# Ten weight blocks decoded later and one at a time, and the low halves of split weights pinned to VectorE, in an attention, mixture-of-experts and feed-forward kernel

## The chip, the cores and the metric

One core of one Trainium2 chip. The metric is the time of one execution in microseconds (us), taken on the device; lower is better. Three timed runs of the kernel before gave 780.74, 778.58 and 780.11 us, median 780.11 us.

The engines that matter here: TensorE (PE, with its weight loads as PEld), VectorE (DVE), ScalarE (ACT), GpSimd (POOL), and the DMA queue that SyncE (SP) issues.

## The reference, cut to what matters

Three stages in a row: clustered attention, a top-1 mixture of experts (MoE), and a dense two-layer block with the activation `h * tanh(softplus(h))`. The change touches only the last one.

```python
def _moe2_setup():
    n_tokens, d_model, d_ff = (1536, 512, 2048)
    return {..., 'w_in': np.random.randn(d_model, d_ff).astype(np.float32) * (1.0 / np.sqrt(d_model)),
                 'w_out': np.random.randn(d_ff, d_model).astype(np.float32) * (1.0 / np.sqrt(d_ff))}

def _moe2_ref(x, w_in, w_out):
    h = x @ w_in
    sp = np.where(h > 20.0, h, np.log1p(np.exp(np.minimum(h, 20.0))))
    g = h * np.tanh(sp)
    return (g @ w_out).astype(np.float32)
```

The product with a numpy scalar makes `w_in` and `w_out` 64-bit floats, so the kernel has to turn them into 32-bit floats itself: that is the decode of which this document speaks.

## The kernel before, in words

**The last part.** The hidden width of 2048 is cut into 16 chunks of 128 columns (`F2 = 16`), and the 1536 tokens into two halves of 768. That makes 32 steps, n = 0 to 31; step n works on chunk `fc = n % 16` of half `n // 16`. Chunk fc has two weight blocks of 128x512, `WD[fc][0]` (from `w_in`) and `WD[fc][1]` (from `w_out`). Each step has, on the different engines:

- `f_split`: each of its two blocks is split into a high and a low part. ScalarE casts the block to `wh` (L1291), then the low part is `wl = WD - wh` (a subtraction recorded at the helper's line L1238). `wh` and `wl` come from the pools `mwh0` and `mwh1`, four pairs each.
- `f_in`, twice (i = 0, 1, for 384 tokens each): 12 matmuls into a PSUM tile `fps` (L1691); then the activation as a chain between VectorE and ScalarE: L1706 (VectorE, reads `fps`), L1709 (ScalarE, exp), L1712 (VectorE), L1717 (ScalarE, ln), L1720 (VectorE, reads `fps` for the last time), L1723 (ScalarE, exp), L1727 (VectorE, multiplies), L1730 (ScalarE, casts to the high half of `g`), L1238 (VectorE, `g` low half). There are two `fps` tiles, so TensorE can begin `f_in` i of step n+1 only when L1720 of `f_in` i of step n is done.
- `f_out`: 18 matmuls of 128x512 from `g`, `wh` and `wl` into six accumulators `ops` (L1766).

TensorE runs them in the order `f_in`(n+1, 0), `f_in`(n+1, 1), `f_out`(n).

**The decode.** A block (`d_block`) is loaded by a DMA that SP issues (L1516, tile `draw`, three buffers), scaled on GpSimd (L1521), its magnitude taken on ScalarE (L1527), then three instructions on VectorE (L1534 clamp, L1540 shifts, L1547 sign merged in), and one addition on GpSimd (L1554) that writes `WD`. There are 32 blocks. The first 22 (`NB = 22`) are decoded while the attention and MoE parts still run; blocks 22 to 31, that is chunks 11 to 15, are decoded inside the last part, since `WD` has memory of its own for only 11 chunks, and chunks 11 to 15 use buffers that become free when the MoE part is done.

**What sets the order.** A planner (`Plan`) lays out all instructions with due times (`at2`) and estimated durations, and writes every engine's queue in that order; each queue is then run strictly in order. An instruction may have alternatives (`alts`): the planner then picks the engine that it thinks finishes first. `sub` is the helper that makes the subtractions; without `psum=True` it offers VectorE and GpSimd. `split` passes `psum=key[0] != "f"`, so for the last part's weights either engine may be chosen.

Of the kernel before, what the change touches and what calls it, by code (L numbers as in the profile page):

```python
# [28 lines left out]
NB = 22  # L29
# [7 lines left out]
def f32(ap):  # L37
    return ap.bitcast(F32)
# [117 lines left out]
def t_dve(n):  # L156
    return 68 + 1.042 * n


def t_pool(n):  # L160
    return 40 + 2.33 * n
# [7 lines left out]
def cluster_attention__then__moe__then__act_mish_kernel(  # L169
# [103 lines left out]
    for i, cc in enumerate(CAPS):  # L273
# [5 lines left out]
        out=kcaps, in0=caps, scalar1=float(E), scalar2=float(E), op0=ALU.mult, op1=ALU.add  # L279
# [21 lines left out]
    for j in range(2):  # L301
        for part, src in ((0, chi), (1, clo)):
            c0 = part * 32 + j * 16
            nc.vector.tensor_copy(
                out=cbig[64 * j:64 * j + 64, :, c0:c0 + 16],
# [6 lines left out]
    for i in range(2):  # L312
        nc.sync.dma_start(
            out=xw[64 * i:64 * i + 64, :, D:], in_=w_gate.rearrange("(h d) e -> d h e", d=D)
# [503 lines left out]
    key = rp.tile([128, E], F32, name="key")  # L818
# [411 lines left out]
                    )  # L1230
                    rest(at_r, at_c, e, px, pw, ps1, ps2)

    def sub(out, in0, in1, deps, n, psum=False, pool=False, **kw):

        def f(eng="dve"):
            e = nc.vector if eng == "dve" else nc.gpsimd
            a, b_, c = out(), in0(), in1()
            e.tensor_tensor(out=a, in0=b_, in1=c, op=ALU.subtract)  # L1238
        alts = [("dve", t_dve(n))] * (not pool) + [("pool", t_pool(n))] * (not psum)
        return O(None, 0, f, deps, alts=alts, **kw)  # L1240

    moe = scope()
# [39 lines left out]
            ms["ld", s, fc, a] = o  # L1282
            after = [ms[0]["ld", t] for t in range(3)] + [o] if (s, fc) == (0, 0) else [o]

    def split(a, key, src, dep, prev, rel=(), pool=False):

        y = ms["wh", key, a] = [None, None]

        def act():
            y[0], y[1] = (mwh[a].tile([128, 512], F32R, tag=x, name=x) for x in ("wh", "wl"))  # L1290
            nc.scalar.copy(out=y[0], in_=src())  # L1291

        o = ms["sa", key, a] = O("act", 520, act, [dep, prev], acq=[(f"mwh{a}", key)])
        ms["sp", key, a] = sub(
            lambda: y[1], src, lambda: f32(y[0]), [o], 512, psum=key[0] != "f", rel=rel, pool=pool,
        )

    def e_split(s, fc):
        for a in range(2):
            if ms[s]["full"]:  # L1300
                ms["sp", (s, fc), a] = ms["ld", s, fc, a]
                continue
            split(a, (s, fc), lambda a=a: ms["w", s, fc, a], ms["ld", s, fc, a],
                  ms["sa", (s, fc), 0] if a else None, [(f"mwr{a}", (s, fc))])

    def e_xt(s, t):
# [29 lines left out]
        if z["full"]:  # L1336
# [3 lines left out]
        o = O("act", t_act(DC * n), lambda: nc.scalar.copy(  # L1340
            out=z["xh"][:, :, t0:t0 + n], in_=y["ps"]), [o])
        z["xt", t] = sub(
            lambda: z["xl"][:, :, t0:t0 + n], lambda: y["ps"],
            lambda: f32(z["xh"][:, :, t0:t0 + n]), [o], DC * n, psum=True, rel=[R],
# [228 lines left out]
    def at2(n, off=0.0):  # L1573
        plan.key = base_k + n * TS + off
# [5 lines left out]
    for n, (s, fc) in enumerate(steps):  # L1580
# [16 lines left out]
        if fc == NF - 1:  # L1597
            if s == 0:
                at2(5)
                o = O("dve", 1000, starts, [begun], after=[ms[0]["y", 2]])  # L1600
# [13 lines left out]
    for blk in range(NB):  # L1614
        if blk < ND0:
            n = (2 * blk + 1) * NF0 // (2 * ND0)
        else:
            n = NF0 - 1 + (blk - ND0) * (NS - 3 - NF0) // (NB - ND0)
# [10 lines left out]
    for b in range(B):  # L1629
# [36 lines left out]
        out=ids, in_=ids_d[:, 0:1].rearrange("(t p) o -> p (t o)", p=128)), ci + [ms[E - 1]["mm1", 0]])  # L1666
# [7 lines left out]
    def f_split(n):  # L1674
        half, fc = divmod(n, F2)
        for a in range(2):
            split(a, ("f", n), lambda a=a: WD[fc][a], dd[2 * fc + a], fs["hold"])
            fs["hold"] = ms["sa", ("f", n), a]

    def f_in(n, i):  # L1680
# [48 lines left out]
        def e8():  # L1729
# [14 lines left out]
        o = O(None, 0, e7, [o, o1], alts=[("dve", t_dve(384)), ("pool", t_pool(384))])  # L1744
        o = O("act", 413, e8, [o])
        fs["e", n, i] = sub(
            lambda: y["gl"], lambda: y["t"], lambda: f32(y["gh"]), [o], 384, rel=[W]
        )
# [69 lines left out]
    for n in range(NM):  # L1818
        at2(n - 2, 1.0)
        f_split(n)  # L1820
        if n < NM - 2:
            for i in range(2):
                at2(n - 1, 2.0 * i)
                f_in(n, i)

            for blk in range(NB, 2 * F2):
                if int((blk - NB) * 0.65 + 2) == n:
                    at2(n - 1, 2.5)
                    d_block(blk, [fs["in"]])
            f_out(n)  # L1830
# [41 lines left out]
```

## Time and profile before

| | |
|---|---|
| median of three runs | 780.11 us (778.58 to 780.74) |
| the profiled execution | 783.48 us |
| its span, first to last instruction | 781.5 us |
| mean granted TensorE clock over the span | 0.975 |
| TensorE busy | 746.9 us (96% of the span) |
| VectorE busy | 565.2 us (72%) |
| ScalarE busy | 476.8 us (61%) |
| GpSimd busy | 232.3 us (30%) |
| last part | about 491 to 774 us of the span |
| decode of blocks 22 to 31 on VectorE | 516 to 572 us of the span |

The shares of the whole span mix stages with different limits. The stage that the change touches has to be read by itself, step by step: a step of the last part begins, in this text, where VectorE starts L1706 of `f_in`(n, 0), and it ends where the next one starts.

Times of instructions include a tail of about 0.08 us that the next instruction on the same engine overlaps; what an instruction takes of a queue is the distance from its start to the start of the next, which is called its slot here.

### The profile page before, as it was taken

What the parts mean: (1) busy time and instruction counts of PE and PEld (TensorE: products, weight loads), DVE (VectorE), ACT (ScalarE), POOL (GpSimd) and SP (SyncE); (2) the same over time, 40 slices, a digit from 0 to 9 for tenths busy, and PEclk for the clock granted to TensorE, in tenths of its full rate; (3) what the DMA queues carried; (4) which work ended last, traced back from release to release, by engine and by line L of the source; (5) the groups of instructions that cost most, each with busy time, mean ns of one, the idle gap of its engine ahead of it and who ended that gap; (6) DMA issues with size and microseconds to landing.
All of it is one profiled execution on the core that took longest, in us unless ns stands there. A gap on an engine that the chain in (4) does not pass through costs nothing.

```text
span 781.5 us, 14002 instructions
## 1 busy us (share of the span) xinstructions
PE 746.9 (96%) x4809; PEld 707.7 (91%) x4810; DVE 565.2 (72%) x1114; ACT 476.8 (61%) x1053; POOL 232.3 (30%) x457
## 2 busy tenths in 40 slices
PE   7999999999999959999999999999899999999995
PEld 6999999999999958999999999988679999999894
DVE  6697887888888855787533333599987778777763
ACT  3587878878788864556433232565556666665644
POOL 2225345358543340144223333125420011000003
PEclk9699999999999988999999999999999999999998
DMA  8949486474541028778688999212100001000002
GB/s 177 216 97 227 113 227 145 136 164 147 117 101 34 1 95 259 229 195 238 206 258 269 300 308 287 78 55 81 55 1 0 1 20 63 0 1 1 1 1 81
DMA packets 96082, 97.34 MB, mean 125 GB/s; under 512 B 33053, under 2 KB 76061, under 8 KB 94981
## 3 DMA queue, kind: packets, MB, share of 16 engines
q1 hardware_dynamic: 92133, 88.91, 41.9%
q0 software_dynamic: 2304, 7.08, 2.4%
q8 instruction: 40, 0.66, 0.4%
q10 hardware_dynamic: 1568, 0.39, 0.3%
q14 instruction: 37, 0.30, 0.1%
HBM read 63.59 MB, written 12.32 MB: 97 GB/s over the span
## 4 chain that ended last, share of the span: by engine, by line
PE 27%; issue 26%; DVE 5%; POOL 1%; DMA 1%; ACT 1%; SPq 0%; POOLq 0%
PE hps L1366 6%; PE yps L1427 6%; PE hps L1350 5%; PE yps L1350 5%; PE fps L1691 2%; PE ops L1766 1%; POOL out_dram L1797 1%; DVE dm L1547 1%; DVE ft L1712 1%; PE tps L1326 1%; DVE ft L1727 1%; DMA wr<-in_moe_w_dram 1%; DVE ft L1706 1%; DMA win<-xs_dram 1%; DVE g L1238 0%
## 5 line engine op out<-in xcount | busy, mean ns | idle before, releaser
L1766 PE MATMUL ops<-wh,g 128*128 128x512 f32 x384 | 125.0, 392 | 0.7 <-ACT g L1730 0.7
L651 DVE TENSOR_REDUCE mn<-sps 128x1 f32<-128x768 f32 x96 | 91.4, 954 | 24.7 <-PE sps L644 23.5
L689 ACT CAST ph<-pt 128x512 fp32r<-128x512 f32 x144 | 81.8, 590 | 29.5 <-PE pt L680 28.7
L692 DVE TENSOR_TENSOR pl<-pt,ph 128x512 fp32r<-128x512 f32 x144 | 95.0, 684 | 5.2 <-ACT ph L689 3.7
L1691 PE MATMUL fps<-YH,wh 128*128 128x384 f32 x256 | 88.8, 347 | 7.9 <-DVE ft L1720 7.9
L655 ACT ACTIVATE p<-sps,mn 128x768 f32<-128x768 f32 x96 | 87.4, 911 | 3.4 <-DVE mn L651 2.9
L1691 PE MATMUL fps<-YL,wh 128*128 128x384 f32 x256 | 87.2, 340 | 0.0
L1691 PE MATMUL fps<-YH,wl 128*128 128x384 f32 x256 | 87.1, 340 | 0.0
L1766 PEld LDWEIGHTS ops<-wh,g 128*128 128x128 f32 x384 | 72.4, 189 | 16.1 <-ACT g L1730 1.1
L680 PE MATMUL pt<-ident,p 128*128 128x128 f32 x576 | 79.1, 275 | 0.4 <-ACT o L787 0.4
L1766 PE MATMUL ops<-wl,g 128*128 128x512 f32 x192 | 75.3, 392 | 0.0
L640 PE MATMUL sps<-asm 128*128 128x384 f32 x192 | 73.9, 385 | 0.0
L680 PEld LDWEIGHTS pt<-ident,p 128*128 128x128 f32 x576 | 68.4, 143 | 2.9 <-ACT o L787 0.5
L1797 POOL DMA_INDIRECT out_dram<-fo,ids x12 | 12.0, 1004 | 188.5 <-ACT fo L1791 120.7
L644 PE MATMUL sps<-asm 80*128 80x384 f32 x192 | 66.8, 348 | 0.0
L1717 ACT ACTIVATE ft<-ft,two 128x384 f32<-128x384 f32 x64 | 39.5, 617 | 41.5 <-DVE ft L1712 41.5
L1366 PE MATMUL hps<-xf,wr 128*128 128x232 f32 (+4 forms) x320 | 59.5, 329 | 1.4 <-DMA wr<-in_moe_w_dram 1.4
L1709 ACT ACTIVATE ft<-ft 128x384 f32<-128x384 f32 x64 | 33.6, 524 | 44.0 <-DVE ft L1706 43.7
L1691 PEld LDWEIGHTS fps<-YH,wh 128*128 128x128 f32 x256 | 48.8, 191 | 12.3 <-DVE ft L1720 11.4
L1554 POOL TENSOR_TENSOR WD<-dm,draw 128x512 int32<-128x512 int32 x32 | 42.5, 1330 | 55.1 <-DVE dm L1547 49.2
L1427 PE MATMUL yps<-hf,wr 128*128 128x232 f32 (+4 forms) x320 | 58.8, 327 | 0.0
L1238 DVE TENSOR_TENSOR wl<-WD,wh 128x512 fp32r<-128x512 f32 x56 | 38.5, 688 | 25.6 <-ACT wh L1291 25.5
(190 smaller groups left out, 1767.2 us busy)
## 6 DMA issues: line engine op xcount, KB each, us to landing
wr<-in_moe_w_dram SPq DMA_DIRECT2D x128, 256.0 KB
asm<-raw SPq DMA_DIRECT2D x16, 576.0 KB
draw<-in_moe_w_in_dram SPq DMA_DIRECT2D x16, 512.0 KB
draw<-in_moe_w_out_dram SPq DMA_DIRECT2D x16, 512.0 KB
asm<-raw SPq DMA_DIRECT2D x16, 384.0 KB
xs_dram<-zrow SPq DMA_DIRECT2D x16, 256.0 KB
vl<-in_v_dram SPq DMA_DIRECT2D x8, 384.0 KB
asm<-raw SPq DMA_DIRECT2D x16, 192.0 KB
```

Of the source, the lines that this page charges most:

```text
L640: nc.tensor.matmul(ps[:, half, :384], a[:, 1, c * 128:(c + 1) * 128], a[:, 0, sl], start=True, stop=False,)
L644: nc.tensor.matmul(ps[:, half, :384], a[:80, 2, c * 128:(c + 1) * 128], a[:80, 3, sl], start=False, stop=True,)
L651: nc.vector.tensor_reduce(out=y["mn"], in_=y["ps"][:, :, :384], axis=AX.XY, op=ALU.min)
L655: nc.scalar.activation(out=p.rearrange("p (a b) -> p a b", a=2), in_=y["ps"][:, :, :384], func=AF.Exp, bias=y["mn"], scale=-1.0, accum_out ...
L680: nc.tensor.transpose(ps[:, kk * 256 + u * 128:kk * 256 + u * 128 + 128], z["p", u][:, kc * 128:(kc + 1) * 128], ident,)
L689: nc.scalar.copy(out=v("ph"), in_=y["ps"])
L692: nc.vector.tensor_tensor(out=v("pl"), in0=y["ps"], in1=f32(v("ph")), op=ALU.subtract)
L1350: nc.tensor.matmul(ps, l, x[:, i], start=first and n == 0, stop=last and n == 2)
L1366: nc.tensor.matmul(ps, w[:, k * 128:(k + 1) * 128], z["x"][:, k, :cap], start=k == 0, stop=k == DC - 1,)
L1427: nc.tensor.matmul(z["y"][d], w[:, d * 128:(d + 1) * 128], h, start=fc == 0 and d % yd == 0, stop=fc == NF - 1 and (d + 1) % yd == 0,)
L1691: nc.tensor.matmul(ps[:, :384], l, r[:, k, c0:c0 + 384], start=(k == 0 and m == 0), stop=(k == DC - 1 and m == 2),)
L1766: nc.tensor.matmul(fs["o", t], l[:, sl], r, start=(fc == 0 and m == 0), stop=(fc == F2 - 1 and m == 2),)
```

## The change

Two edits. The ten blocks inside the last part were placed at step `int((blk - 22) * 0.65 + 2)`, that is at steps 2, 2, 3, 3, 4, 5, 5, 6, 7, 7; now at `int((blk - 22) * 1.2 + 2)`, steps 2, 3, 4, 5, 6, 8, 9, 10, 11, 12. And `split` always passes `psum=True`, so that `wl` is always made by VectorE. (The argument `pool` that goes away was never set.)

```diff
-    def sub(out, in0, in1, deps, n, psum=False, pool=False, **kw):
+    def sub(out, in0, in1, deps, n, psum=False, **kw):
...
-        alts = [("dve", t_dve(n))] * (not pool) + [("pool", t_pool(n))] * (not psum)
+        alts = [("dve", t_dve(n))] + [("pool", t_pool(n))] * (not psum)
...
         ms["sp", key, a] = sub(
-            lambda: y[1], src, lambda: f32(y[0]), [o], 512, psum=key[0] != "f", rel=rel, pool=pool,
+            lambda: y[1], src, lambda: f32(y[0]), [o], 512, psum=True, rel=rel,
         )
...
             for blk in range(NB, 2 * F2):
-                if int((blk - NB) * 0.65 + 2) == n:
+                if int((blk - NB) * 1.2 + 2) == n:
                     at2(n - 1, 2.5)
                     d_block(blk, [fs["in"]])
```

VectorE's queue in step 4, where before two blocks are decoded and now one; `dm` is the block in decode, `ft` the activation's tile, `fps` the PSUM tile. Before:

```order
L1540 TENSOR_SCALAR dm<-dm 128x512
L1706 TENSOR_SCALAR ft<-fps 128x384
L1547 SCALAR_TENSOR_TENSOR dm<-draw,dm 128x512
L1534 TENSOR_SCALAR dm<-dm 128x512
L1712 SCALAR_TENSOR_TENSOR ft<-ft 128x384
L1540 TENSOR_SCALAR dm<-dm 128x512
L1706 TENSOR_SCALAR ft<-fps 128x384
L1547 SCALAR_TENSOR_TENSOR dm<-draw,dm 128x512
L1720 TENSOR_TENSOR ft<-fps,ft 128x384
L1712 SCALAR_TENSOR_TENSOR ft<-ft 128x384
```

The last two instructions of one block and all three of the next stand among the activation's here. The same place now:

```order
L1540 TENSOR_SCALAR dm<-dm 128x512
L1706 TENSOR_SCALAR ft<-fps 128x384
L1547 SCALAR_TENSOR_TENSOR dm<-draw,dm 128x512
L1238 TENSOR_TENSOR wl<-WD_0_4674,wh 128x512
L1712 SCALAR_TENSOR_TENSOR ft<-ft 128x384
L1706 TENSOR_SCALAR ft<-fps 128x384
L1720 TENSOR_TENSOR ft<-fps,ft 128x384
L1712 SCALAR_TENSOR_TENSOR ft<-ft 128x384
```

The second block's three instructions are gone from between the first L1706 and the first L1720, and the `wl` of chunk 7, which GpSimd made, stands there instead.

GpSimd's queue in the last part, from the first `wl` on; `draw` is a loaded block, `WD_7545` and the like are decoded blocks. Before:

```order
L1238 TENSOR_TENSOR wl<-WD_0_4668,wh 128x512
L1521 TENSOR_SCALAR draw<-draw 128x512 x2
L1238 TENSOR_TENSOR wl<-WD_0_4672,wh 128x512
L1554 TENSOR_TENSOR WD_7545<-dm,draw 128x512
L1554 TENSOR_TENSOR WD_7567<-dm,draw 128x512
L1521 TENSOR_SCALAR draw<-draw 128x512 x2
L1238 TENSOR_TENSOR wl<-WD_0_4674,wh 128x512
L1554 TENSOR_TENSOR WD_7638<-dm,draw 128x512
L1554 TENSOR_TENSOR WD_7661<-dm,draw 128x512
```

Each `wl` stands between a pair of L1521 and the L1554 that write the decoded blocks. The same place now:

```order
L1521 TENSOR_SCALAR draw<-draw 128x512
L1554 TENSOR_TENSOR WD_7543<-dm,draw 128x512
L1521 TENSOR_SCALAR draw<-draw 128x512
L1554 TENSOR_TENSOR WD_7622<-dm,draw 128x512
L1521 TENSOR_SCALAR draw<-draw 128x512
L1554 TENSOR_TENSOR WD_7705<-dm,draw 128x512
```

The eight `wl` have left the queue (they stand in VectorE's now), and L1521 and L1554 alternate instead of coming in pairs. SP's queue of DMAs is the same in both kernels, and TensorE's differs in one place: in step 1, three `f_out` matmuls now stand before a group of twelve `f_in` matmuls instead of behind it.

## Rows read from the trace of the kernel before

**Rows 1.** Page, busy time of each engine over the span
```profile
PE 746.9 (96%) x4809; PEld 707.7 (91%) x4810; DVE 565.2 (72%) x1114; ACT 476.8 (61%) x1053; POOL 232.3 (30%) x457
```

**Rows 2.** Busy time by stretch: us; engines' busy; granted clock (PEclk), DMA share, GB/s
```profile
core 0: us, PE busy (x) PEld busy (x) DVE busy (x) ACT busy (x) POOL busy (x), PEclk, DMA share, GB/s
...
509.91:596.51 86.60, 78.90 (x375) 69.73 (x374) 79.45 (x130) 50.66 (x98) 30.67 (x25) 0.96 0.14 43
...
588.20:638.04 49.84, 49.84 (x254) 45.49 (x253) 38.40 (x73) 30.56 (x60) 0.00 (x0) 1.00 0.00 1
...
528.63:538.44 9.81, 7.87 (x32) 6.89 (x31) 9.70 (x15) 4.84 (x10) 4.78 (x4) 0.83 0.35 107
538.44:548.82 10.38, 10.38 (x55) 9.48 (x54) 10.05 (x18) 6.87 (x15) 6.29 (x6) 1.00 0.15 52
...
578.28:588.20 9.92, 9.92 (x44) 8.98 (x43) 6.95 (x14) 5.79 (x11) 0.00 (x0) 0.83 0.01 2
```

**Rows 3.** TensorE: waits in the last part (total, times, longest), then single matmuls
```profile
PE fps L1691 <- DVE ft L1720: 7.9, 7, 1.9
...
534.25 0.44 PE L1691 MATMUL fps<-YH,wh 128*128 128x384 f32 x1 [1.94 <-DVE ft L1720]
554.44 0.44 PE L1691 MATMUL fps<-YH,wh 128*128 128x384 f32 x1 [1.69 <-DVE ft L1720]
577.75 0.45 PE L1691 MATMUL fps<-YH,wh 128*128 128x384 f32 x1 [1.90 <-DVE ft L1720]
...
602.28 0.33 PE L1691 MATMUL fps<-YH,wh 128*128 128x384 f32 x1
```

**Rows 4.** VectorE in step 11, without decode: start, duration, [idle before, releaser]
```profile
596.51 0.55 DVE L1706 TENSOR_SCALAR ft<-fps 128x384 f32<-128x384 f32 x1
597.65 0.56 DVE L1712 SCALAR_TENSOR_TENSOR ft<-ft 128x384 f32<-128x384 f32 x1 [0.59 <-ACT ft L1709]
...
598.90 0.56 DVE L1720 TENSOR_TENSOR ft<-fps,ft 128x384 f32<-128x384 f32 x1
...
603.13 0.69 DVE L1238 TENSOR_TENSOR wl<-WD,wh 128x512 fp32r<-128x512 f32 x1 [0.81 <-ACT wh L1291]
...
604.21 0.68 DVE L1238 TENSOR_TENSOR wl<-WD,wh 128x512 fp32r<-128x512 f32 x1
604.81 0.55 DVE L1706 TENSOR_SCALAR ft<-fps 128x384 f32<-128x384 f32 x1
```

**Rows 5.** VectorE in step 6, with decode
```profile
548.82 0.55 DVE L1706 TENSOR_SCALAR ft<-fps 128x384 f32<-128x384 f32 x1
549.28 1.31 DVE L1547 SCALAR_TENSOR_TENSOR dm<-draw,dm 128x512 uint32<-128x512 uint32 x1
550.52 0.41 DVE L1534 TENSOR_SCALAR dm<-dm 128x512 f32<-128x512 f32 x1
550.85 1.66 DVE L1712 SCALAR_TENSOR_TENSOR ft<-ft 128x384 f32<-128x384 f32 x1
...
553.24 0.68 DVE L1547 SCALAR_TENSOR_TENSOR dm<-draw,dm 128x512 uint32<-128x512 uint32 x1
553.84 0.55 DVE L1720 TENSOR_TENSOR ft<-fps,ft 128x384 f32<-128x384 f32 x1
554.30 1.46 DVE L1712 SCALAR_TENSOR_TENSOR ft<-ft 128x384 f32<-128x384 f32 x1
555.69 1.00 DVE L1727 TENSOR_TENSOR ft<-ft 128x384 f32<-128x384 f32 x1
```

**Rows 6.** GpSimd in step 6
```profile
548.58 1.47 POOL L1238 TENSOR_TENSOR wl<-WD,wh 128x512 fp32r<-128x512 f32 x1 [2.55 <-ACT wh L1291]
550.74 1.35 POOL L1554 TENSOR_TENSOR WD<-dm,draw 128x512 int32<-128x512 int32 x1 [0.69 <-DVE dm L1547]
554.06 1.30 POOL L1554 TENSOR_TENSOR WD<-dm,draw 128x512 int32<-128x512 int32 x1 [1.96 <-DVE dm L1547]
555.44 0.85 POOL L1521 TENSOR_SCALAR draw<-draw 128x512 uint32<-128x512 uint32 x1
```

More of the change, by code (lines that the diff above doesn't have):

```diff
@@ L1283, in e_load, with split @@
             after = [ms[0]["ld", t] for t in range(3)] + [o] if (s, fc) == (0, 0) else [o]
-    def split(a, key, src, dep, prev, rel=(), pool=False):
+    def split(a, key, src, dep, prev, rel=()):
         y = ms["wh", key, a] = [None, None]
```

## The prediction

> **What bounds the kernel now.** I read the busy shares first: TensorE is at work for 96% of the span [rows 1], so what there is to win lies in the few stretches where it stands still or runs slowly. Then I cut the last part into steps, each from one first L1706 to the next. From 588.20 to 638.04 us there are six steps without decode: 49.84 / 6 = 8.307 us each, TensorE busy throughout, clock 1.00, VectorE busy 38.40 of 49.84 us [rows 2]. That is the pace that TensorE sets. The nine steps from 509.91 to 596.51 us, in which the ten blocks are decoded, take 86.60 us [rows 2] where nine clean ones would take 9 x 8.307 = 74.76. So the decode inside the last part costs 86.60 - 74.76 = **11.84 us**, and this is all that the change can win back; nothing else in the kernel is touched.
>
> Where the 11.84 go: TensorE waits seven times, 7.9 us in all, each time for L1720, the instruction that lets go of a PSUM tile `fps` [rows 3]. Two of the longest waits (1.94 and 1.90 us) are followed by a lower clock: 0.83 over the steps at 528.63 and at 578.28 [rows 2, 3], a mixture of the two levels 2.4 and 1.2 GHz. That costs 9.81 x 0.17 + 9.92 x 0.17 = 3.4 us. Waits and clock make 11.3 of the 11.84. After a wait of 1.69 us no such step follows [rows 2, 3].
>
> Why L1720 is late: VectorE's queue is too long in these steps. In step 6 no row shows idle time ahead of an instruction, and several of its instructions are stretched while GpSimd runs: L1712 takes 1.66 instead of 0.56 us over GpSimd's L1554, L1547 1.31 instead of 0.68 over GpSimd's `wl`, L1727 1.00 instead of 0.55 over L1521 [rows 4 to 6]. L1706 and L1720, which read PSUM, are not stretched under the same GpSimd instructions (0.55 each) [rows 5, 6].
>
> **The move of `wl`.** Eight subtractions leave GpSimd and each adds a slot of 604.81 - 604.21 = 0.60 us to VectorE [rows 4]: 4.8 us. But each on GpSimd also held VectorE up by 1.31 - 0.68 = 0.63 us [rows 5], 5.0 us for eight. I take the move as neutral for VectorE's queue; its ends are +4.8 us of queue, if nothing comes back, and a gain of some 4 us if the stall is as long as L1712's under L1554 (1.10). As for place: `wl` of part 0 now stands between L1706 and L1712 of the first `f_in`, where VectorE waits 0.59 us for ScalarE's exp anyway [rows 4]. ScalarE has the same work as before, and the three matmuls that change places in step 1 I cost at nothing: TensorE has both groups ready, and without that cover it is at most their own time, about half a microsecond.
>
> **The stretching of the decode.** No instruction is added or taken away; ten blocks are spread over steps 3 to 7 and 9 to 13 (where their L1547 stands), one each, step 8 without. What counts is the length of VectorE's queue in such a step. Slots: an instruction on 384 columns 554.30 - 553.84 = 0.46, say 0.47; L1547 553.84 - 553.24 = 0.60; L1534 and L1540 550.85 - 550.52 = 0.33 [rows 5]. One step is then:
>
> - ten instructions of the activation, 10 x 0.47 = 4.70;
> - L1547 and two `wl`, 3 x 0.60 = 1.80; L1534 and L1540, 0.66;
> - one hit by L1554: GpSimd starts it when the `wl` behind L1547 ends, and the next in VectorE's queue is L1712, which it stretched by 1.66 - 0.56 = 1.10 [rows 4, 5];
> - no hit by L1521: it follows L1554 at once on GpSimd (555.44 after 554.06 + 1.30), and now L1706 and L1720 stand there, which read PSUM;
> - two waits of L1720 for ScalarE's ln: 1.25 us lie between starts of L1712 and L1720 [rows 4], two slots fill 0.94, so 2 x 0.31 = 0.62.
>
> Sum 8.88 us, against TensorE's 8.307: VectorE falls behind by 0.57 us a step. The hit and the ln waits are the uncertain items. Without either the step is 7.2 us and nothing is lost; if L1521 hits as well, by 1.00 - 0.55 = 0.45 [rows 4, 5], it is 9.33 and VectorE loses 1.02 a step. I take the middle because every L1554 in the rows does hit a L1712, and both L1521 and PSUM readers are seen passing each other.
>
> What it may fall behind: in a clean step TensorE begins the next `f_in` 602.28 - 596.51 = 5.77 us after L1706 [rows 3, 4], and it can begin 0.60 us after L1720 has started (553.84 and 554.44) [rows 3, 5]. In the new step L1720 starts 0.47 + 0.60 + 0.60 + 0.47 + 1.10 + 0.47 + 0.31 = 4.02 us after L1706. Slack: 5.77 - 0.60 - 4.02 = 1.15 us. So in steps 3 to 7 TensorE waits 4 x 0.57 - 1.15 = 1.1 us. Step 8 has no L1547 and VectorE catches up the 0.81 us that it otherwise waits for `wh` [rows 4]; from there the second five steps cost 5 x 0.57 - 0.81 = 2.0. In general, with d the loss per step, 9 x d - 1.96: **3.2 us** of waits, each well below the 1.90 that preceded a slow clock, so that the 3.4 us of clock come back too.
>
> **Other things moved.** The blocks' DMAs keep their order on SP's queue and have three buffers; with one block a step they are asked for less often. The last decode now ends near step 13; chunk 15 is first needed by TensorE's `f_in` of step 15, so a step (8.3 us) is left. L1554 of block 30 has to wait for a `wh`/`wl` pair of `mwh1`, which holds GpSimd's queue, and behind it only block 31's L1554; ScalarE's cast of block 30 waits behind that. If the cover of a step were used up, the wait would fall on TensorE once, some microseconds.
>
> **Sum.** 11.84 - 3.2 = 8.6 us gained. Against the profiled execution, 783.48 - 8.6 = 774.9; that execution lies 3.4 us above the median of the runs, and I carry the gain over unchanged: 780.11 - 8.6 = **771.5 us**. A measurement of this kernel tells about 0.3%, 2.3 us, from no change.
>
> **The rivals.**
>
> *All comes back.* GpSimd's hits fall into VectorE's waits for ScalarE; d is 0.2 or less, so 9 x d - 1.96 is nothing, time 780.11 - 11.84 = 768.3. For it: (49.84 - 38.40) / 6 = 1.9 us of 8.307 are idle on VectorE in clean steps [rows 2]. Against it: every L1554 in rows 5 and 6 costs. Chance 0.17.
>
> *L1521 hits too, or a lower clock follows once.* d = 1.02 gives 7.2 us of waits, 775.5; a lower clock after one wait adds 1.7 (9.92 x 0.17). Together 777.2 at most. For it: now there are ten single L1521, where pairs shared one hit. Against it: where they stand. Chance 0.15.
>
> *Each GpSimd instruction costs VectorE its whole length.* VectorE is blocked for 1.30 by L1554 and 0.85 by L1521 [rows 6] in every step: d = 0.57 + (1.30 - 1.10) + 0.85 = 1.62, waits 12.6, time 780.9: no change, the same loss only spread over more steps. Against it: L1706 and L1720 ran at 0.55 over such instructions [rows 5, 6]. Chance 0.06. The Trainium skill's page "SBUF — State Buffer", section "Who interferes with whom", states the rule behind this: a VectorE instruction with two SBUF inputs and a GpSimd instruction that reads SBUF exclude each other for a whole instruction, and whichever starts first blocks the other. It also says that an instruction with at most one SBUF input, outside the two-port modes, does not contend, and the rows on L1706 and L1720 agree; by that part of the page L1521 finds nothing to block where it now stands.
>
> *Slower.* VectorE stays the bound for eleven steps instead of nine, each as long as the step at 538.44, which had a single L1547 and still took 10.38 us [rows 2]. Then d = 2.07, waits 16.7, time 785.0. It would be slower by over 0.3% from d = 1.8, a step of 10.1 us. For it: that row. Against it: two of GpSimd's `wl` ran in that step, and these are what the change takes away. Chance 0.05.
>
> That the change does not do what it says is excluded by the queues shown: `wl` is gone from GpSimd's, and the blocks are apart.
>
> **How the numbers follow.** The forecast (769.5 to 774.5) has 0.57, and the rivals 0.17, 0.15, 0.06 and 0.05. The range goes from 768.0, nothing lost, to 777.0, which takes in the hit by L1521 and one slow clock; outside it lie the last two and a little of the third. Faster by over 0.3%: 0.57 + 0.17 + 0.15 = 0.89; no change 0.06; slower 0.05.
>
> **What would show it.** Right: steps 3 to 13 of 8.3 to 8.9 us; waits of TensorE for L1720 of about 3 us in all, none above 1.2, at the ends of the two groups of five; clock 1.00 throughout; L1712 still stretched, once a step; L1547 at 0.68 everywhere. Wrong: L1727 or the `g` subtractions stretched as well, waits above 1.5 us with a clock below 1.00 after them, steps over 9.3 us, or TensorE waiting for `wl` of chunk 15 near step 15.

## The result and the profile after

The changed kernel takes **768.46 us** (median of four runs, 767.84 to 771.49), beside 779.85 us for the kernel before (four runs, 778.58 to 780.74). The ratio is 0.9857 with a 95% interval of 0.9840 to 0.9875: faster by 11.4 us, where 8.6 us and 771.5 us were forecast. The profiled execution took 767.84 us.

The page's busy times, to set against [rows 1]:

```profile
span 766.1 us, 14014 instructions
...
PE 741.1 (97%) x4809; PEld 704.1 (92%) x4810; DVE 559.0 (73%) x1122; ACT 474.6 (62%) x1053; POOL 223.4 (29%) x449
```

Eight instructions moved from GpSimd to VectorE, as said, and yet VectorE was busy for less time than before (559.0 for 565.2 us): its instructions were stretched less. TensorE's waits, and then the first matmuls of four of its `f_in` groups, among them the one behind the only wait that is left, to set against [rows 3]:

```profile
PE fps L1691 <- DVE ft L1720: 0.2, 1, 0.2
...
520.04 0.33 PE L1691 MATMUL fps<-YH,wh 128*128 128x384 f32 x1
...
544.96 0.33 PE L1691 MATMUL fps<-YH,wh 128*128 128x384 f32 x1
...
553.66 0.44 PE L1691 MATMUL fps<-YH,wh 128*128 128x384 f32 x1 [0.23 <-DVE ft L1720]
...
603.62 0.35 PE L1691 MATMUL fps<-YH,wh 128*128 128x384 f32 x1
```

Seven waits of 7.9 us have become one of 0.23 us, in step 7. Then the steps with decode, each from one first L1706 to the next, in the columns of [rows 2]:

```profile
core 0: us, PE busy (x) PEld busy (x) DVE busy (x) ACT busy (x) POOL busy (x), PEclk, DMA share, GB/s
...
514.02:522.68 8.66, 8.66 (x46) 7.93 (x45) 8.26 (x17) 5.71 (x12) 2.38 (x2) 1.00 0.20 62
522.68:531.56 8.88, 8.88 (x47) 8.15 (x46) 8.45 (x16) 5.45 (x11) 2.39 (x2) 1.00 0.19 59
531.56:539.71 8.15, 8.15 (x43) 7.42 (x42) 7.82 (x16) 5.57 (x11) 3.06 (x2) 1.00 0.19 65
539.71:548.59 8.88, 8.88 (x47) 8.15 (x46) 8.45 (x16) 5.45 (x11) 2.44 (x2) 1.00 0.21 62
548.59:557.46 8.87, 8.63 (x45) 7.56 (x44) 8.66 (x16) 5.37 (x10) 2.15 (x2) 1.00 0.18 59
557.46:564.73 7.27, 7.27 (x38) 6.54 (x38) 6.25 (x15) 5.50 (x11) 0.00 (x0) 1.00 0.00 0
...
582.48:590.63 8.15, 8.15 (x43) 7.43 (x42) 7.82 (x16) 5.05 (x10) 3.88 (x3) 1.00 0.00 0
590.63:598.89 8.26, 8.26 (x44) 7.53 (x43) 7.48 (x15) 5.23 (x10) 1.67 (x1) 1.00 0.01 3
...
506.33:622.80 116.47, 116.23 (x588) 105.66 (x587) 108.05 (x200) 75.20 (x149) 24.49 (x19) 1.00 0.10 32
```

These are steps 3 to 8, 11 and 12, and then steps 2 to 15 in one. The fourteen steps take 116.47 us, and at TensorE's pace of 8.307 they would take 116.30. So of the loss of 11.84 us in the decode of before, 0.17 is left, and the granted clock is 1.00 all along where it fell to 0.83 twice. The 11.67 us that came back are the 11.4 by which the medians differ, to within the measurement. (The two profiled spans differ by more, 15.4 us; the rest lies ahead of this part, in instructions that are the same, and before's profiled execution was 3.4 us above its median.)

VectorE's queue in steps 4, 5 and 7 of after, for [rows 5] (start, duration, idle before):

```profile
523.15 0.68 DVE L1547 SCALAR_TENSOR_TENSOR dm<-draw,dm 128x512 uint32<-128x512 uint32 x1
523.75 0.69 DVE L1238 TENSOR_TENSOR wl<-WD,wh 128x512 fp32r<-128x512 f32 x1
524.35 1.67 DVE L1712 SCALAR_TENSOR_TENSOR ft<-ft 128x384 f32<-128x384 f32 x1
525.94 0.55 DVE L1706 TENSOR_SCALAR ft<-fps 128x384 f32<-128x384 f32 x1
526.70 0.56 DVE L1720 TENSOR_TENSOR ft<-fps,ft 128x384 f32<-128x384 f32 x1 [0.22 <-ACT ft L1717]
...
533.23 0.55 DVE L1712 SCALAR_TENSOR_TENSOR ft<-ft 128x384 f32<-128x384 f32 x1
...
534.47 0.56 DVE L1720 TENSOR_TENSOR ft<-fps,ft 128x384 f32<-128x384 f32 x1 [0.22 <-ACT ft L1717]
...
535.41 1.00 DVE L1727 TENSOR_TENSOR ft<-ft 128x384 f32<-128x384 f32 x1
...
550.12 1.49 DVE L1712 SCALAR_TENSOR_TENSOR ft<-ft 128x384 f32<-128x384 f32 x1
551.53 1.13 DVE L1238 TENSOR_TENSOR wl<-WD,wh 128x512 fp32r<-128x512 f32 x1
...
553.06 0.55 DVE L1720 TENSOR_TENSOR ft<-fps,ft 128x384 f32<-128x384 f32 x1
```

And GpSimd's in steps 4 and 5, for [rows 6]:

```profile
524.07 1.54 POOL L1554 TENSOR_TENSOR WD<-dm,draw 128x512 int32<-128x512 int32 x1 [5.26 <-DVE dm L1547]
525.68 0.85 POOL L1521 TENSOR_SCALAR draw<-draw 128x512 uint32<-128x512 uint32 x1
532.86 2.10 POOL L1554 TENSOR_TENSOR WD<-dm,draw 128x512 int32<-128x512 int32 x1 [6.32 <-DVE dm L1547]
535.04 0.97 POOL L1521 TENSOR_SCALAR draw<-draw 128x512 uint32<-128x512 uint32 x1
```

Step 4 is the step of the forecast: L1547 runs at 0.68, L1712 behind it takes 1.67 over L1554, and L1521 (525.68 to 526.53) leaves no mark on the L1706 that runs beside it (0.55) and is over before L1720 starts. Step 5 has the same instructions in the same order up to there, and is 0.73 us shorter: here L1712 runs at 0.55, and it is L1554 that lasts longer, 2.10 us. L1521 then comes later in the step and stretches L1727 to 1.00.

### The profile page after: what moved, and what is told of

Read it like the earlier page. It is cut to its first block, busy times and chain, and to the rows that moved or that the text cites. A ratio compares the mean times of both kernels' runs of the same rounds, so it can differ in the third digit from the quotient of the medians.

```text
span 766.1 us, 14014 instructions
## 1 busy us (share of the span) xinstructions
PE 741.1 (97%) x4809; PEld 704.1 (92%) x4810; DVE 559.0 (73%) x1122; ACT 474.6 (62%) x1053; POOL 223.4 (29%) x449
## 4 chain that ended last, share of the span: by engine, by line
PE 27%; issue 21%; DVE 8%; ACT 2%; DMA 2%; POOL 1%; SPq 1%; POOLq 0%; ACTq 0%
PE hps L1366 7%; PE yps L1427 7%; PE yps L1350 5%; PE hps L1350 5%; PE fps L1691 2%; DVE ft L1712 2%; PE ops L1766 1%; DVE wl L1238 1%; DMA wr<-in_moe_w_dram 1%; ACT ft L1717 1%; POOL out_dram L1797 1%; DVE ft L1720 1%; DVE ft L1727 1%; PE tps L1326 1%; DVE ft L1706 1%
## 5 line engine op out<-in xcount | busy, mean ns | idle before, releaser
L1691 PE MATMUL fps<-YH,wh 128*128 128x384 f32 x256 | 87.2, 340 | 0.3 <-DVE ft L1720 0.2
L1691 PE MATMUL fps<-YL,wh 128*128 128x384 f32 x256 | 86.1, 336 | 0.0
L1691 PE MATMUL fps<-YH,wl 128*128 128x384 f32 x256 | 86.1, 336 | 0.0
L1554 POOL TENSOR_TENSOR WD<-dm,draw 128x512 int32<-128x512 int32 x32 | 45.2, 1413 | 127.8 <-DVE dm L1547 87.2
L1238 DVE TENSOR_TENSOR wl<-WD,wh 128x512 fp32r<-128x512 f32 x64 | 44.5, 695 | 19.9 <-ACT wh L1291 19.8
L1366 PEld LDWEIGHTS hps<-xf,wr 128*128 128x128 f32 x320 | 52.6, 190 | 1.6 <-DMA wr<-in_moe_w_dram 1.1
```

The lines of the kernel that those rows point to most:

```text
L1366: nc.tensor.matmul(ps, w[:, k * 128:(k + 1) * 128], z["x"][:, k, :cap], start=k == 0, stop=k == DC - 1,)
L1691: nc.tensor.matmul(ps[:, :384], l, r[:, k, c0:c0 + 384], start=(k == 0 and m == 0), stop=(k == DC - 1 and m == 2),)
```

## The experiments

The theory: GpSimd's instructions stretch VectorE's two-input instructions; with 1.5 blocks to a step VectorE's queue is then longer than TensorE's step, TensorE waits for L1720, and two of those waits bring the low clock. One block a step fits into the step and the slack. The rivals: the move of `wl` off GpSimd does it; or VectorE's own decode instructions, not GpSimd's, make the queue too long. The kernel before took 780.68 us beside the first four kernels, and 780.44 beside the last three.

### Each edit alone

The spacing alone, in the kernel before:

```diff
-                if int((blk - NB) * 0.65 + 2) == n:
+                if int((blk - NB) * 1.2 + 2) == n:
```

> The ten blocks at 1.2 steps apart, but the planner may still put wl on GpSimd (it puts ten of them there). Theory (VectorE's queue length per step, with GpSimd's hits in it): a wl on GpSimd stretches one L1547 by 0.63 us, a wl on VectorE takes 0.60, so the move is neutral and the spreading alone gives the whole gain: 767.5 to 770 us, waits of TensorE for L1720 below 1 us, clock 1.00 in the last part. Rival (the pinning matters by itself, since a wl of 1.3 to 1.5 us on GpSimd can also land on a L1712 or a g subtraction and cost 1.1 each): steps longer by about 0.5, 771 to 775 us, with L1547, L1540 or g stretched in the trace.

Measured: 769.51 us (767.44 to 770.43), ratio 0.9863 (0.9838 to 0.9888). Nine steps of that kernel, by stretch, and then two groups of VectorE's instructions in the decode (count, busy time, mean ns of one, idle time before):

```profile
513.95:588.76 74.81, 74.81 (x380) 68.29 (x379) 69.94 (x125) 50.05 (x97) 32.18 (x25) 1.00 0.16 50
```

```profile
L1712 DVE SCALAR_TENSOR_TENSOR ft<-ft 128x384 f32<-128x384 f32 x26 | 14.3, 551 | 2.0 <-ACT ft L1709 1.8
...
L1547 DVE SCALAR_TENSOR_TENSOR dm<-draw,dm 128x512 uint32<-128x512 uint32 x10 | 12.6, 1264 | 0.0
```

These are steps 3 to 11, all but step 8 with one block. 74.81 / 9 = 8.31 us a step: TensorE's own pace, with nothing lost; its two waits for L1720, 0.5 us together, lie outside these steps. With ten `wl` on GpSimd the stretching is not gone, it sits elsewhere: nine of the ten L1547 take 1.31 to 1.42 instead of 0.68 us, the L1727 over L1521 take 1.00, and no L1712 is stretched (551 ns). A step with decode is thereby shorter for VectorE than in the kernel after, 8.31 us against 34.57 / 4 = 8.64 in steps 3 to 6 there; both are hidden, so the times are alike.

The move of `wl` alone, with the old spacing, in the kernel after:

```diff
-                if int((blk - NB) * 1.2 + 2) == n:
+                if int((blk - NB) * 0.65 + 2) == n:
```

> The ten blocks at 0.65 steps apart as before, wl on VectorE only. Theory: neutral move, so the loss of the kernel before stays: 777.5 to 781 us, waits of TensorE for L1720 of 6 to 9 us with a lower clock after the longest. Rival (pinning brings a good part of the gain): 770 to 776 us.

Measured: 778.48 us (774.76 to 781.12, twelve runs), ratio 0.9971 (0.9951 to 0.9992). TensorE's waits and its longest:

```profile
PE fps L1691 <- DVE ft L1720: 5.6, 5, 2.7
...
555.98 0.44 PE L1691 MATMUL fps<-YH,wh 128*128 128x384 f32 x1 [2.65 <-DVE ft L1720]
```

The ten microseconds around it, by stretch:

```profile
555.00:565.00 10.00, 9.03 (x38) 8.50 (x39) 9.20 (x18) 6.29 (x13) 3.32 (x3) 0.83 0.13 48
```

The move alone is worth 2.2 us, just beyond what can be told from nothing; 5.6 us of waits, a little under the 6 to 9 expected, and a stretch at 0.83 are still there. Spreading alone is worth 11.2, as much as both together. So the gain is the spacing's.

### No GpSimd in the decode, at the old spacing

As the kernel above, but in the last ten blocks L1521 and L1554 are left out, and L1547 writes the decoded block itself. VectorE keeps its three instructions per block, ScalarE and the DMAs keep theirs. The low bits of these blocks are missing.

```diff
-        o1 = O("pool", t_pools(512) + 100, p1, [o])
+        o1 = o if blk >= NB else O("pool", t_pools(512) + 100, p1, [o])
...
+            if blk >= NB:
+                place()
+                m = WD[fc][part].bitcast(U32)
...
+        if blk >= NB:
+            dd[blk] = O("dve", t_dve(512), d4, [o], rel=[R], acq=W, after=[dd.get(blk - 1)])
+            return
```

> As e2_pin_only (0.65 steps apart, wl on VectorE only), but the last ten blocks leave out GpSimd's two instructions: L1521 and L1554 are gone for them and L1547 writes the decoded block itself, so the low bits of these ten blocks are missing from the result. Theory: what makes the queue too long is GpSimd's hits; without them a two-block step is 10 x 0.47 + 4 x 0.60 + 4 x 0.33 + 0.62 = 9.04 us, a one-block step 7.8, and the lag stays below the slack: 767.5 to 770 us, no L1712 above 0.6 us, next to no waits for L1720. Rival (VectorE's own decode instructions, 10 x 1.26 = 12.6 us, are what delays L1720 whether or not GpSimd runs): 773 to 779 us, waits of 3 us or more.

Measured: 769.70 us (766.00 to 771.64), ratio 0.9852 (0.9823 to 0.9880). TensorE's waits (lines stand eight lower in this kernel: L1699 is L1691, L1728 is L1720):

```profile
PE fps L1699 <- DVE ft L1728: 0.2, 1, 0.2
```

That wait lies behind the decode. VectorE's L1712, which is L1720 here:

```profile
L1720 DVE SCALAR_TENSOR_TENSOR ft<-ft 128x384 f32<-128x384 f32 x25 | 13.7, 552 | 3.1 <-ACT ft L1717 2.6
```

One instruction is left on GpSimd beside the decode, a `g` subtraction, and it stretches the one L1547 (L1552 here) that it meets, 0.68 us long elsewhere:

```profile
517.12 1.40 POOL L1238 TENSOR_TENSOR g<-ft,g 128x384 fp32r<-128x384 f32 x1 [29.62 <-ACT g L1738]
...
517.56 1.51 DVE L1552 SCALAR_TENSOR_TENSOR WD<-draw,dm 128x512 uint32<-128x512 uint32 x1
```

Eight blocks are decoded in the five steps 2 to 6 here (the last two only in step 12), with VectorE's three instructions for each and all the `wl` in its queue, and nothing is lost. So VectorE's own decode work is not what made the queue too long: the second rival falls as it stands. One thing moved with GpSimd's instructions, because the planner laid out the queues anew: in steps 3, 4 and 6 the second block's L1547 stands behind both L1720, while in steps 3, 4 and 6 of the kernel before both stood ahead of the first. That the order alone would not have done it is argued and not shown: in the kernel before, the first L1720 of step 6 starts 5.02 us after L1706, and without the hits of 0.63 and 1.10 us ahead of it that would be 3.29, which by the prediction's 5.77 and 0.60 us leaves a slack of 1.88.

### How near the edge: 1.0, 1.4, and the kernel after again

```diff
-                if int((blk - NB) * 1.2 + 2) == n:
+                if int((blk - NB) * 1.0 + 2) == n:
```

> The changed kernel with the ten blocks exactly one step apart, so that no step without decode lies among them. Theory (lag adds up over successive decode steps, and only what exceeds a slack of 1.15 us is waited for): the changed kernel lost 1.9 us of lag in five steps, so ten in a row lose 3.8, waits of 2 to 3 us at the end of the row, 770 to 772 us, clock 1.00. Rival (a step with one block is harmless by itself, only two in one step cost): no waits, 768 to 769 us.

Measured: 769.64 us (768.18 to 771.40), ratio 0.9859 (0.9834 to 0.9884). The waits, 2 to 3 us of which were expected, and the matmul behind the only one:

```profile
PE fps L1691 <- DVE ft L1720: 0.2, 1, 0.2
...
557.17 0.44 PE L1691 MATMUL fps<-YH,wh 128*128 128x384 f32 x1 [0.23 <-DVE ft L1720]
```

Eight steps from 517.55 us on, by stretch, and then two of GpSimd's L1554 in them:

```profile
517.55:586.22 68.67, 68.44 (x347) 62.19 (x346) 65.76 (x122) 44.70 (x89) 21.20 (x17) 1.00 0.17 54
```

```profile
536.38 2.10 POOL L1554 TENSOR_TENSOR WD<-dm,draw 128x512 int32<-128x512 int32 x1 [6.32 <-DVE dm L1547]
...
579.39 2.07 POOL L1554 TENSOR_TENSOR WD<-dm,draw 128x512 int32<-128x512 int32 x1 [6.35 <-DVE dm L1547]
```

The expectation missed. With no step left out to recover in, VectorE should have lost d each step and run out of slack. Eight steps cost it 68.67 - 8 x 8.307 = 2.2 us, 0.28 each and not 0.57, since L1712 is spared in four of them: in two L1554 lasts 2.1 us, as in step 5 of after, and in two it starts only behind the first L1712.

The other way, 1.4, which places the ten blocks at steps 2, 3, 4, 6, 7, 9, 10, 11, 13 and 14 (each L1547 stands one step later):

```diff
-                if int((blk - NB) * 1.2 + 2) == n:
+                if int((blk - NB) * 1.4 + 2) == n:
```

> The changed kernel with the blocks 1.4 steps apart (steps 2, 3, 4, 6, 7, 9, 10, 11, 13, 14), so that chunk 15 is decoded only just before TensorE needs it. Theory: no run of more than three decode steps, so no waits for L1720; but the wl of block 30 now ends about 5.8 us into step 14 and TensorE wants it at 6.0, so 0 to 2 us are lost there: 768 to 771 us. Rival (the late decode bites, through the instructions queued behind the casts and subtractions of chunk 15 on ScalarE and VectorE): a wait of TensorE of 3 to 8 us near steps 14 to 16, 772 to 777 us.

Measured: 768.12 us (767.54 to 768.40), ratio 0.9846 (0.9820 to 0.9871), and no wait for L1720 at all. The kernel after once more beside it, unchanged:

> The changed kernel once more, as the measure for the two beside it: 767.5 to 770 us, waits of TensorE for L1720 of 0.2 to 0.5 us, step times of 8.1 to 8.9 us.

Measured: 769.18 us (769.02 to 770.08), ratio 0.9861 (0.9836 to 0.9886), with one wait of 0.2 us as before. The intervals of the two overlap; there is no version here that clearly beats the kernel after, and a decode that ends two steps later does not make TensorE wait for its last chunks.

### A longer queue on purpose

In the kernel after, L1547 is issued twice for each of the ten blocks (the second writes the same bits). That was meant to add 0.60 us to VectorE's queue in each such step and nothing anywhere else.

```diff
-            nc.vector.scalar_tensor_tensor(
-                out=m, in0=y["t"][:, :, 1], scalar=0xC0000000, in1=m, op0=ALU.bitwise_and,
-                op1=ALU.bitwise_or,
-            )
+            for _ in range(2 if blk >= NB else 1):
+                nc.vector.scalar_tensor_tensor(
+                    out=m, in0=y["t"][:, :, 1], scalar=0xC0000000, in1=m, op0=ALU.bitwise_and,
+                    op1=ALU.bitwise_or,
+                )
```

> The changed kernel with the third decode instruction of VectorE (L1547 there) issued twice for each of the ten blocks; it writes the same bits again. Each decode step's queue grows by one slot of 0.60 us, and the slack between L1720 and TensorE's next f_in shrinks by the same 0.60, to 0.55 us. Theory (queue length and slack): from the steps of the changed kernel the lag of steps 3 to 6 is 1.34 + 4 x 0.60 = 3.7, less 0.55 makes waits of 3.2 us; step 8 gives 1.0 back; steps 9 to 12 make 0.67 + 0.93 + 2.4 less 0.55 = 3.4 us: 6 to 7 us of waits in all, 774 to 776 us, and more if one of them is long enough for a lower clock. Rival (one block a step stays hidden whatever it is, since TensorE is the bound): under 1 us of waits, 768 to 770 us.

Measured: 776.12 us (775.02 to 780.46, twelve runs), ratio 0.9958 (0.9941 to 0.9975), 6.9 us above the kernel after beside it and just over the 774 to 776 expected. TensorE's waits (lines stand one lower) and the longest:

```profile
PE fps L1692 <- DVE ft L1721: 6.2, 6, 1.4
...
557.21 0.44 PE L1692 MATMUL fps<-YH,wh 128*128 128x384 f32 x1 [1.44 <-DVE ft L1721]
```

The doubled L1547 and what follows it, and then steps 3 to 13 of this kernel and of the kernel after, by stretch:

```profile
523.10 1.41 DVE L1548 SCALAR_TENSOR_TENSOR dm<-draw,dm 128x512 uint32<-128x512 uint32 x2
524.42 0.69 DVE L1238 TENSOR_TENSOR wl<-WD,wh 128x512 fp32r<-128x512 f32 x1
```

```profile
513.42:615.01 101.59, 95.29 (x474) 84.78 (x473) 96.11 (x172) 58.74 (x118) 22.85 (x19) 1.00 0.12 37
...
514.02:607.81 93.79, 93.56 (x474) 85.15 (x473) 88.56 (x161) 59.25 (x118) 24.49 (x19) 1.00 0.12 40
```

The two instructions take 524.42 - 523.10 = 1.32 us of the queue, so the second added 0.72 and not 0.60; and in steps 5 and 11, where the kernel after has L1712 spared (8.15 us), it is hit here (9.60 and 9.59). Together VectorE's eleven steps are 101.59 - 93.79 = 7.8 us longer. Counted by its own first `f_in` matmuls, TensorE takes 99.69 us for eleven steps here (519.43 to 619.12) and 91.92 in the kernel after (520.04 to 611.96): 7.8 us more as well. It waits 6.0 us more, and the same 474 matmuls take 95.29 - 93.56 = 1.7 us longer at a clock of 1.00, some 0.3 for each of the six waits: a wait cost more than the idle time that is shown. So all that was added to VectorE's queue was paid by TensorE: the kernel after stands at the edge of its slack, and next to nothing of it is left over in either row of five. It also shows that the loss goes by the length of the queue, whatever makes it long. That the waits came to the 6 to 7 us expected is in part luck, since the expectation had a smaller addition.

## Why the prediction was right, and where its sum was off

**The loss to be won back** (11.84 us) was right: 0.17 us is left in fourteen steps, and the whole gain is 11.4 us. That waits and clock make nearly all of it fits the kernel without GpSimd's decode, where both are gone and 11.0 us with them. The sum priced a wait at its idle time alone, though; with the doubled L1547 each wait cost some 0.3 us more.

**The move of `wl` as neutral** was right at the new spacing: 769.51 us without it, 768.46 and 769.18 with it. At the old spacing it is worth 2.2 us, within the bounds given (4.8 us of cost, 4 of gain). At the new spacing it is neutral only because both kernels hide their decode: VectorE's steps are 8.31 us long without the move and 8.64 with it.

**The step of 8.88 us** was right to the hundredth where its items came together: steps 4 and 6 have 8.88. So L1547 at 0.68, L1712's hit, no hit by L1521, and the waits for ln were each as costed. (The prediction says that L1521 and PSUM readers were seen passing each other; the rows that it names show them passing `wl` and L1554 only. In the kernel after L1521 passes L1706.)

**The term that was mis-sized** is "one hit by L1554" taken for every step, and so d = 0.57 in 9 x d - 1.96. Six of the ten L1554 hit a L1712 (1.49 to 1.67 us, steps 4, 6, 7, 9, 10 and 13). In steps 3, 5 and 11 L1712 was not hit, and L1727 was, by L1521 (1.00 us): for steps 5 and 11 that is 8.88 - 1.10 + 0.45 = 8.23, measured 8.15. In step 12 L1554 started only at 595.61, 4.98 us into the step, and fell on a `g` subtraction (1.68 us for 0.56), behind both L1720; the step took 8.26. The four distances from step 3 to step 7 sum up to 34.57 us, which is 34.57 - 4 x 8.307 = 1.34 of loss, where 4 x 0.57 = 2.28 was forecast. By TensorE's pace the matmuls after 544.96 were due at 544.96 + 8.31 = 553.27, which by the forecast's 5.77 belongs to a L1706 at 547.50; the real one was at 548.59, so VectorE had fallen behind by 1.09 us. (It came into step 3 some 0.25 ahead: TensorE's matmuls at 520.04 follow L1706 at 514.02 by 6.02 us, not 5.77.) Step 7's own slack was not the forecast's 1.15: its L1720 starts 553.06 - 548.59 = 4.47 us after L1706, not 4.02, because L1712 (1.49) and `wl` (1.13) were both hit. That leaves 5.77 - 0.60 - 4.47 = 0.70, and 1.09 - 0.70 = 0.39 us is how late the matmuls at 553.66 are; the trace shows 0.23 of it as idle. TensorE's pace and the 0.60 us from L1720's start to the matmul (553.06 and 553.66) hold here; what was off were the lag and step 7's own L1720.

**Step 8** gives back 8.307 - 7.27 = 1.04 us, not 0.81. With that, and with the two shorter steps of the second row of five, the forecast's 2.0 us of waits there became none: L1720 of step 13 starts at 602.90 and lets go 0.60 later, at 603.50, just ahead of the matmuls at 603.62, which did not wait.

So 0.2 us of waits came in place of 3.2, and the time is 3.0 us below 771.5. It lies in the range, but below the 769.5 to 774.5 that got the chance of 0.57, and so does the kernel after once more (769.18); it fell to the first rival's 768.3, which got 0.17. That rival was right on the time, but its reason, that the hits would fall into VectorE's waits for ScalarE, is only part of it: six hits on L1712 still cost 0.9 to 1.1 us each, and the slack and step 8 took them in. Two of the prediction's own signs came out against it: L1712 was not stretched in every step, and L1727 (three times) and a `g` subtraction (once) were. The other three rivals fall all the same: no clock fell, and no step came near 10 us. TensorE did not wait for chunk 15.

## What to carry to other kernels

Work that is to be hidden beside a bound engine should be spread so that each step's queue, its hits by other engines counted, fits into that step and its slack; the same ten blocks cost 11.8 us at 1.5 a step and nothing at one a step. Cost such a step by its queue on the helper engine, not by busy shares: 0.72 us more per step was hidden no longer. Where two engines hinder one another, either spread their meetings, or put instructions that do not collide (here those that read PSUM) where the other engine will run.

## What the runs showed of the hardware

Which of the two gives way is not fixed. L1554 over L1712 lasts 1.54 us and L1712 1.67 in step 4; in step 5 L1554 lasts 2.10 and L1712 0.55. In both, L1554 is recorded as starting while `wl`, a two-input instruction, still runs (0.32 and 0.23 us after its start), and L1712 follows `wl` at once. The recorded start does not decide it: in step 10 L1554 also starts 0.23 us after `wl`, and L1712 takes 1.66. Nor does the kernel: in the unchanged kernel's second profile the same steps 5 and 6 have it the other way round.

```profile
535.11 1.61 POOL L1554 TENSOR_TENSOR WD<-dm,draw 128x512 int32<-128x512 int32 x1 [6.32 <-DVE dm L1547]
535.48 1.66 DVE L1712 SCALAR_TENSOR_TENSOR ft<-ft 128x384 f32<-128x384 f32 x1
...
544.00 2.07 POOL L1554 TENSOR_TENSOR WD<-dm,draw 128x512 int32<-128x512 int32 x1 [6.35 <-DVE dm L1547]
544.35 0.55 DVE L1712 SCALAR_TENSOR_TENSOR ft<-ft 128x384 f32<-128x384 f32 x1
```

The Trainium skill, "SBUF — State Buffer", section "Who interferes with whom", says that the order of issue decides which one blocks the other for its whole instruction; neither outcome contradicts that. Which comes first when both wait behind a third, neither a trace nor a run here tells, and it stays open. It moves a step by 0.73 us.

Of waits of TensorE for L1720, those of 1.94 and 1.90 us in the kernel before and of 2.65 us at the old spacing with `wl` on VectorE lie in or just ahead of a stretch at a granted clock of 0.83; those of 1.69 us in before and of 1.44 us with the doubled L1547 do not: the clock stayed at 1.00. From the first `f_in` matmul behind such a wait to that of the next step TensorE took 9.97 us in the kernel before (534.25 to 544.22) and 9.97 at the old spacing (555.98 to 565.95), where the kernel after took 8.42 behind its 0.23 us of wait (553.66 to 562.08) at 1.00: the low clock cost 1.55 us each time, near the 1.7 of the prediction's sum. So short waits came cheaper than a few long ones: 6.2 us of them made VectorE's steps 7.8 us longer in the one kernel, 7.9 us made them 11.84 longer in the other.
